# An MLP's down product by Strassen's seven products in place of eight, inside a fused RWKV-7 + MLP kernel

## The chip, the cores and the metric

The kernel runs on one core of one Trainium2 chip. The metric is the device time of one execution in microseconds: 678.31 us is the median of three runs of the kernel before (677.22 to 678.55). Engines are named as in the profile: PE (TensorE, matmul), PEld (its weight loads), DVE (VectorE), ACT (ScalarE), POOL (GpSimd), SP (the queue that issues all DMAs here). SBUF is the working memory, PSUM the memory that PE writes.

## The reference

Two stages. The first is a recurrence over 768 steps for 4 batches and 8 heads of 40 channels; its output is laid out as x with 3072 rows (batch and step) and 320 columns (head and channel). The second is an MLP.

```python
for t in range(S):
    y[:, :, t] = einsum('bhd,bhde->bhe', rt, state)
    Sa = einsum('bhde,bhe->bhd', state, at)
    state = state * wt[:, :, None, :] - einsum('bhd,bhe->bhde', Sa, bt) + einsum('bhd,bhe->bhde', vt, kt)
h = x @ w_in                        # 3072x320 @ 320x2048
g = h * sigmoid(1.702 * h)
out = g @ w_out                     # 3072x2048 @ 2048x320
```

All is float32.

## The kernel before

**Units and chunks.** The sequence is cut into 12 chunks of 64 steps. A chunk has two units (two batches each), 24 units in all. For a unit the kernel loads its inputs (`load`, `load_w`), forms the decays (`logarithm`, `decay`; the running sums are two DVE scans, L533 and L534), prepares score matrices (`prep`), inverts a triangular matrix level by level (`inverse`: PE product ps_level; copies W, L751; differences E, L753; transposes, L702 and L723; block spreading, L709 on POOL or DVE, L707 on ACT) and solves and carries the state (`solve`). Its output x, formed at L953 by four products on DVE or POOL, goes to DRAM (L963) and comes back transposed as xT_all (L967). The attention of unit i needs the state of the chunk before, so it is a chain; the MLP of a chunk only needs that chunk's two units.

**The MLP of a chunk.** x of the chunk has 256 rows: row blocks p (two pairs of batches) and b (batch of the pair). `up` makes h transposed, 2048 by 256, in four quarters q; each quarter is 2 x 5 tasks of four matmuls on the four 64x64 quarters of the PE array (`QUARTERS`), 256 columns wide. One ACT instruction (L988) applies the gelu to a quarter and writes g. `down(p)` then accumulates, for each p, 8 parts (m) of 2 x 4 matmuls with 64 columns of g as weights and 320 columns of w_out moving; row half r of the array writes its own PSUM bank r. A copy of bank 0 (L1012, ACT or DVE) and an add of bank 1 (L1014, DVE) give `ob`, which SP stores (L1011). Each float32 matmul of the code shows as two MATMULs and two LDWEIGHTS in the trace; all matmuls have line L300, the helper `mm`.

**PSUM** is used as four pairs of two banks; a task's number behind the engine's letter in the order is its pair. `down(0)` and `down(1)` are two different uses of a pair.

**Weights.** w_in and w_out come as eight 64-bit pieces of 1.31 MB, in four DMAs each (L469), and are rounded to float32 by an ACT, three DVE and one POOL instruction (L447 to L463). Raw pieces wait in `extra`, in not yet used parts of `w_sb`, or in xT_all.

**The order.** Nothing schedules at run time. Each task is added to a `Plan` with the engines that may do it and a cost for each; a task with `"sbuf": True` reads two SBUF operands and may stand on DVE or POOL or on DVE alone. The text `ORDER` names, for every task, its place, its engine (p, a, d, g, s for PE, ACT, DVE, POOL, SP) and its PSUM pair. `listed` reads it, and the tasks are issued in that order; every engine works through its own in sequence.

The buffers that matter: `g` has four slots (one chunk), `ob` one, x one, xT three.

Of the kernel before, what the change touches and what calls it, by code (L numbers as in the profile page):

```python
# [20 lines left out]
ALU = mybir.AluOpType  # L21
# [86 lines left out]
0s 8s 26s 5s 7s 9s 3a 6s 87p0 88p1 24s 89a1 1s 2s 12s 102a 95d 100p2 90a0 93d 158a 101d2 98p3 96g 10s 94d 17s 97g 16s 99d3  # L108
103p1 4a 11s 132p0 104a1 105d1 142p2 143p3 133a0 106d 130p1 14s 144a3 13s 107p0 15s 18s 151g 108a0 109d0 51s 131a1 110p3 27s
149g 150d 111a3 112d3 159p0 156p1 145a2 161d0 160a0 152g 113p3 345s 92a 162d 25s 153d 114a3 163p2 42s 115d3 34s 19a 274s 264p0  # L110
165d2 265p3 164a2 22d 266a3 166p2 20d 273s 21d 33s 43s 167a2 154p3 168d2 23g 35s 28a 157d1 116p2 155d3 169p1 117a2 118d2 267a0
279d 63s 280g 119p3 277s 171d1 36s 44s 123a3 120d3 343s 125d3 121a 278g 124d3 29d 287a 126p2 170a1 288p0 127a2 30d 172p1 479s
122a3 31d 289a0 128p2 54s 173a1 45s 129d2 32g 62s 174d1 134p3 37a 290d0 175p2 344s 135d3 180a2 146s 178a2 275s 176d2 136p1
179a2 38d 181a2 39d 177a 282g 276s 291d 91s 138a1 182p0 188p3 281d 183a0 186p2 139d 137a1 283p0 187a2 184p1 189a3 40d 140s
292p2 46a 60s 284d0 41g 285p3 185d1 148a 286d3 190p0 293a2 294d2 334p1 335p3 357a 191d0 141s 268g 147s 336a3 315d 192p2 47d
337a1 348d 316p0 194a2 346s 295p3 349d 61s 317a0 195g 347s 358p1 296a3 297d3 360d1 318a0 298p3 271a 361d 319p0 338g 300d3 196s
193a2 320a0 355p2 385d 270s 48d 299a3 362p0 356d2 351g 301p3 363a0 364d0 350g 386p2 197s 302d3 365p0 387a2 269s 352g 359a1
303d3 388a2 323p1 367d0 366a0 321p3 49d 324a1 304p2 322a3 478s 325d1 50g 353p0 309a2 470p3 354d0 209p1 307a2 210p1 310a2 305d2
211p1 308a2 272d 198p0 341a 199p0 72s 212p1 70s 64a 200p0 340s 368p2 52s 342d 339s 69s 201p0 369a2 202p0 370d2 203p0 471a
213p1 65d 214p1 389p2 66d 472a3 483g 204p0 390a2 560s 371p3 67d 306a 53s 215p1 71s 482s 216p1 372a3 217p1 476a 220p2 373d3 68g  # L120
218p1 221p2 477d 219a1 205p0 222p2 206p0 223p2 224p2 78s 559s 207p0 55a 311p3 225p2 79s 312d3 80s 226p2 208a0 58d 313p1 374p3
314d1 227p2 56d 379a3 228p2 229p2 57d 326p0 230a2 59g 393p1 327d0 378a3 391p2 394a1 375d3 231p0 558s 392d2 376a 232p0 233p0
395d1 81s 73a 234p0 480s 381p2 235p0 474s 328p1 475s 382a2 74d 377a3 485d 380a3 236p0 75d 481s 492a 242p2 486d 243p2 82a 76d
484d 77g 383p3 237p0 384d3 244p2 329d1 330d1 488p3 473d 238p0 531d 245p2 487g 246p2 489d3 85d 532p1 708s 239p0 533a1 396p3
331d 534a1 240p0 247p2 397d3 332s 241a0 562s 535p1 83d 490p3 536a1 84d 398p0 706s 572a 491d3 86g 550p1 253p3 399d0 551a 555s
400d0 561s 333s 254p3 401d 255p3 552a1 564d 493p0 402s 556a 567g 570p1 554s 494d0 248p2 705s 563d 566g 249p2 495d0 498d 256p3
571d1 565g 403s 250a2 496a0 251d2 696p1 497g 557d 539p0 252s 537p2 257p3 538a2 704s 540d0 701s 258p3 553d 611d 697a 499d 573p2
259p3 576a2 574d2 784s 710d 700s 260p3 787s 541d0 575d2 404p0 578d 261a3 577g 405p0 579d 698a1 568p2 711g 500p1 406p0 569d2
501a1 407p0 262d3 580p2 702a 502d1 263s 408p0 582d2 409p0 503d 410p0 583d 504a 612p3 411p0 584g 613d3 412p0 614d3 413p0 505p1
709d 414a0 426p3 506d1 427p3 428p3 507d1 429p3 699d 581d2 430p3 615p1 703d 431p3 616a1 785s 585p0 432p3 508d 586a0 433p3 587d0  # L130
434p3 509a 588d 435p3 589d 448p2 436a3 510p1 590p0 511a1 449p2 592d0 591a0 512d1 415p3 513d 416p3 593d 514a 417p3 594g 418p3
515p0 419p3 516a0 517d0 595p1 518d 420p3 596a1 597d1 421p3 598d 422p3 519a 599d 423p3 424p3 520p0 425a3 437p1 521d0 438p1
523d0 522g 439p1 524d0 440p1 525d0 441p1 442p1 526d0 527p3 718p0 528a3 443p1 719d0 929s 444p1 720d0 529p3 445p1 721d0 446p1
530d3 600p0 723d 447a1 542p3 722d 724g 603d0 605a0 619p1 604d0 543d3 450p2 620a1 606d0 544p3 621d1 601d0 602d 617p1 707s 546d3
451p2 618a1 783s 712d 547g 713d 607p0 725p1 608a0 452p2 609p0 453p2 548s 610d0 932s 454p2 727d1 726d1 622p0 728d 545d3 729a
775p1 455p2 623d0 780s 776a 549s 756d 730p3 624p0 456d2 457d2 731d3 458s 459p2 777a1 778g 732d3 786s 788g 781a 779s 626d0
460p2 625d0 627g 733d 795p1 835d 734a 461p2 735p3 791g 462p2 628s 736a3 796d1 737d3 716p0 792g 738d 463p2 782d 739g 1011s
920p1 757p3 925s 464p2 717d0 758a3 629s 759a3 790d 465p2 740p0 789d 466p2 741a0 742d0 921a 797p3 467d2 760p0 1008s 468d2 800a3
923d 652p2 469s 761d0 922a1 653p2 926a 930s 798d3 714p1 799d3 654p2 924s 802d 801g 655p2 934d 803a 656p2 836p0 657p2 715d1
658p2 659p2 837d0 762p3 838d0 927d 660p2 763a3 661p2 764p1 662a2 743d 630p0 744d 928s 631p0 632p0 765d1 804p3 766d1 633p0  # L140
805a3 806d3 634p0 807d 635p0 808a 745p2 636p0 748d2 637p0 749d2 839p1 933g 750d2 638p0 840a1 1009s 751d2 639p0 809p3 746d2
935g 640a0 641p1 810d3 642p1 793p2 747a 811d3 674p0 812d 794d2 813a 752p3 643p1 753a3 814p2 644p1 815a2 816d2 754p3 645p1
755d3 646p1 817d 647p1 818a 767p2 841p3 768d2 648p1 842a3 649p1 819p2 650p1 820a2 821d2 769p3 822d 651a1 823d 675p0 771d3 931s
770d3 772g 824p2 936d 676p0 827a2 828a2 942p1 829a2 677p0 1153s 830a2 937d 945a1 773s 663p3 825d2 664p3 943d1 1156s 826a 665p3
944d1 999p2 947d 946g 666p3 1000a 1004s 980d 940p1 948g 667p3 941d1 668p3 774s 669p3 670p3 831p1 671p3 1001a2 1002d 1003s
832d1 672p3 1005a 1013d 678p0 673a3 1006d 833p2 843p1 679p0 834d2 1007s 844d1 938p2 845d1 680p0 939d2 846p3 681p0 847d3 949p1
1012g 682d0 848p2 950a1 683d0 1014d 684s 685p3 849d2 1015g 1010s 850d2 1021p0 1016g 951d1 686p3 1024a0 1232s 851d 1235s 981p2
687p3 982a2 952d 852s 1022d0 983a2 953g 1144p1 1023d0 688p3 1026d 1145a 1149s 1025d 1027g 984p2 1059d 689p3 1154s 954p0 853s
985a2 1147g 690p3 1158d 1148s 955a0 956d0 986p2 1146a1 957d 1150a 691p3 958d 987a2 1151d 988p0 692p3 989a0 1152s 990d0 959p1
693a3 865p2 960a1 694d3 866p2 961d1 867p2 695s 962d 868p2 963d 1028p0 869p2 1029a0 1030d0 870p2 1031d 1157g 871p2 1159d 1032a  # L150
1060p3 872p2 873p2 1061a3 874p2 1062d3 1033p1 875a2 854p0 1035d1 855p0 1036d 856p0 1037d 1063p3 857p0 1064d3 1034a1 858p0
964p2 859p0 965a2 966d2 1038p1 967d 860p0 1039a1 1040d1 861p0 1041d 1017p3 968a 1042g 862p0 1018d3 863p0 969p2 864a0 876p1
970d2 877p1 972d2 971g 1043p3 973d2 878p1 1044a3 974d2 879p1 975d2 880p1 881p1 1045d3 1019p0 1046d 976p2 1047a 882p1 1020d0
1233s 883p1 977a2 1166p3 884p1 1169a3 1167d3 1377s 978p0 885p1 1168d3 898p2 1171d 1170g 886a1 979d0 887p3 1172a 1048p0 991p1
1051a0 888p3 1052a0 992d1 889p3 1053a0 890p3 1054a0 891p3 1049d0 993p1 1050a 1067p0 994d1 1160g 1155s 892p3 1161d 1068a0 893p3
894p3 1069d0 1380s 895p3 1204d 1065p0 995d1 896p3 996d 1066a0 1231s 1055p1 899p2 897a3 1056d1 997s 1173p0 1223p3 900p2 1174a0
1175d0 1228s 1176d 1224a 1177g 1057p1 901p2 1058d1 1070p0 998s 1164p1 1225a3 1226d 1236g 1227s 1071d0 902p2 1229a 1165d1
1162p3 903p2 1238d 1163d3 904p2 1237d 1178p0 1230d 905p2 1179a0 1180d0 1245p1 906a2 1181d 1072p3 1248a1 1456s 907d2 1182g
1246d1 908s 1247d1 909p0 1250d 1234s 1239g 1073d3 1251a 910p0 1240g 1074d3 1249d 1183p2 1459s 1283d 1368p1 911p0 1184a2 1075d
1373s 912p0 1185d2 1369a 1076s 1186d 1252p3 1187d 913p0 1370a1 1371g 1372s 1382d 1253a3 1188p2 1254d3 1374a 914p0 1255d 1190d2  # L160
1256g 1077s 1189a2 1191d 1243p1 1375d 915p0 1192g 1257p3 916p0 1244d1 1258a3 1259d3 1205p2 917d0 1206a2 1193p1 918d0 1207a2
# [87 lines left out]
def rwkv7_gelu_quick(ctx: ExitStack, tc: tile.TileContext, time_d, v_d, w_d, wc_d, ak_d, b_d, rv_d, w_in, w_out, out):  # L249
# [3 lines left out]
    C = 64  # L253
# [11 lines left out]
    PLAIN = 4  # L265
    PARTS = 4
    ROUNDS, WINDOW, SHARE = 4, 5000.0, 1.0
    RANKS = [14, 16, 20, 24, 35, 37, 39, 41]
    HALF = [slice(0, 64), slice(64, 128)]
    CHANNELS = [slice(h.start, h.start + D) for h in HALF]  # L270
    BITS = (0, 1)
# [858 lines left out]
```

## Time and profile before

| | before |
|---|---|
| median of three runs | 678.31 us (677.22 to 678.55) |
| span of the profiled execution | 681.1 us, 2.8 above that median |
| MATMULs of ps_down, 64x320 | 3072, mean 430 ns, union 240.3 us |
| MATMULs of ps_up, 64x256 | 3840, mean 377 ns, union 254.4 us |
| ACT gelu, L988 | 48, mean 1024 ns |
| ACT table loads | 30, 1283 ns each |
| POOL L709 (128x512) | 29, mean 1323 ns; DVE the same 699 ns |
| first ps_up, first ps_down | 69.0, 93.5 us |
| DMA | 69.73 MB, mean 102 GB/s |

How to read it: the busy time of a group is the union of its instructions' spans. Matmuls are pipelined, so that a span of 430 ns says little about how often one can start; the distance from start to start in the timeline says that. A share of busy time is a mean over the whole span, and the stretches of this kernel differ.

### The profile page before, as it was taken

What the parts mean: (1) busy time and instruction counts of PE and PEld (TensorE: products, weight loads), DVE (VectorE), ACT (ScalarE), POOL (GpSimd) and SP (SyncE); (2) the same over time, 40 slices, a digit from 0 to 9 for tenths busy, and PEclk for the clock granted to TensorE, in tenths of its full rate; (3) what the DMA queues carried; (4) which work ended last, traced back from release to release, by engine and by line L of the source; (5) the groups of instructions that cost most, each with busy time, mean ns of one, the idle gap of its engine ahead of it and who ended that gap; (6) DMA issues with size and microseconds to landing.
All of it is one profiled execution on the core that took longest, in us unless ns stands there. A gap on an engine that the chain in (4) does not pass through costs nothing.

```text
span 681.1 us, 42181 instructions
## 1 busy us (share of the span) xinstructions
PE 652.0 (96%) x19488; PEld 572.4 (84%) x19488; DVE 445.5 (65%) x906; ACT 330.7 (49%) x688; POOL 176.7 (26%) x204
## 2 busy tenths in 40 slices
PE   5777999999999999999999999999999999999997
PEld 5667888997987788888888898899899799889996
DVE  4687877777867668767776587868556766675001
ACT  4675845544564654664545445455454354252110
POOL 5443444225123123123123211321412421300000
PEclk9788999999999999999999999999999999999999
DMA  7874755205314314432404413513502312200100
GB/s 235 275 244 148 228 158 173 89 14 155 108 50 139 103 45 125 124 108 67 121 23 131 140 34 107 154 33 106 149 29 71 121 51 58 58 13 23 51 12 21
DMA packets 35312, 69.73 MB, mean 102 GB/s; under 512 B 5440, under 2 KB 14656, under 8 KB 35136
## 3 DMA queue, kind: packets, MB, share of 16 engines
q1 hardware_dynamic: 35136, 67.03, 32.8%
q8 instruction: 153, 2.51, 1.6%
q14 instruction: 23, 0.19, 0.1%
HBM read 59.15 MB, written 7.86 MB: 98 GB/s over the span
## 4 chain that ended last, share of the span: by engine, by line
PE 91%; DMA 4%; ACT 1%; DVE 1%; issue 1%; SPq 0%; ACTq 0%; DVEq 0%
PE ps_up L300 31%; PE ps_down L300 30%; PE ps_level L300 9%; PE ps_y L300 5%; PE ps_B L300 4%; PE ps_X L300 2%; PE ps_N L300 2%; PE ps_rz L300 2%; PE ps_RV L300 2%; PE ps_A L300 1%; DMA ak<-in_ak 1%; PE ps_zT L300 1%; PE ps_Q L300 1%; DMA time<-in_time 1%; PE ps_T L300 1%
## 5 line engine op out<-in xcount | busy, mean ns | idle before, releaser
L300 PE MATMUL ps_up<-xT_all,w_sb 64*64 64x256 f32 x3840 | 254.4, 377 | 2.0 <-DMA xT_all<-x_dram 1.1
L300 PE MATMUL ps_down<-w_sb,g 64*64 64x320 f32 x3072 | 240.3, 430 | 1.1 <-issue 0.9
L300 PEld LDWEIGHTS ps_up<-xT_all,w_sb 64*64 64x64 f32 x3840 | 172.9, 133 | 17.7 <-issue 2.5
L300 PEld LDWEIGHTS ps_down<-w_sb,g 64*64 64x64 f32 x3072 | 143.3, 133 | 31.4 <-issue 1.6
L988 ACT ACTIVATE g<-ps_up 128x1024 f32<-128x1024 f32 x48 | 49.1, 1024 | 44.7 <-PE ps_up L300 44.3
L709 POOL TENSOR_TENSOR EX<-ES,quads 128x512 f32<-128x512 f32 x29 | 38.3, 1323 | 115.5 <-DVE ES L702 83.1
L751 ACT COPY W<-ps_level 128x512 f32<-128x512 f32 x56 | 32.7, 585 | 69.1 <-PE ps_level L300 67.4
L300 PEld LDWEIGHTS ps_level<-W,EX 64*64 64x64 f32 x2560 | 59.2, 134 | 5.8 <-DVE T L830 0.2
L300 PE MATMUL ps_level<-W,EX 64*64 64x64 f32 (+1 forms) x2560 | 56.2, 217 | 0.0
L753 DVE TENSOR_TENSOR E<-two,ps_level 128x256 f32<-128x256 f32 x80 | 33.1, 415 | 34.7 <-ACT W L751 30.7
L707 ACT ACTIVATE EX<-ES,quads 128x256 f32<-128x256 f32 x80 | 36.3, 501 | 30.4 <-DVE ES L702 29.9
L619 POOL TENSOR_TENSOR ak<-ak,FT 128x512 f32<-128x512 f32 x16 | 22.0, 1378 | 76.2 <-DMA ak<-in_ak 54.4
L300 PE MATMUL ps_level<-PT,EX 64*64 64x64 f32 (+2 forms) x1280 | 34.9, 244 | 5.7 <-DVE EX L723 4.8
L300 PEld LDWEIGHTS ps_level<-PT,EX 64*64 64x64 f32 x1280 | 32.6, 145 | 8.9 <-DVE EX L723 5.7
L702 DVE STREAM_TRANSPOSE ES<-E 128x256 f32<-128x256 f32 x80 | 35.2, 442 | 4.7 <-DVE E L753 0.5
L300 PE MATMUL ps_y<-M,bh 64*64 64x104 f32 (+1 forms) x768 | 34.8, 247 | 1.3 <-DVE M L907 0.8
L300 PE MATMUL ps_y<-RV,kh 64*64 64x104 f32 (+1 forms) x768 | 34.9, 247 | 0.3 <-DVE EX L723 0.3
L891 ACT COPY B<-ps_B 128x416 f32<-128x416 f32 (+1 forms) x34 | 16.5, 492 | 33.5 <-PE ps_B L300 33.2
L300 PEld LDWEIGHTS ps_y<-RV,kh 64*64 64x64 f32 x768 | 28.9, 133 | 2.0 <-DVE M L907 0.5
L907 DVE TENSOR_TENSOR M<-ps_X,later 128x832 f32<-128x832 f32 (+1 forms) x24 | 23.8, 993 | 9.8 <-PE ps_X L300 9.5
L627 POOL TENSOR_TENSOR kh<-time,G 128x320 f32<-128x320 f32 x18 | 16.2, 902 | 48.4 <-PE ps_y L300 34.4
L300 PEld LDWEIGHTS ps_y<-M,bh 64*64 64x64 f32 x768 | 27.0, 133 | 1.9 <-DVE M L907 1.2
(131 smaller groups left out, 1097.2 us busy)
## 6 DMA issues: line engine op xcount, KB each, us to landing
ak<-in_ak SPq DMA_DIRECT2D x48, 160.0 KB
rv<-in_rv SPq DMA_DIRECT2D x48, 160.0 KB
time<-in_time SPq DMA_DIRECT2D x24, 320.0 KB
xT_all<-x_dram SPq DMA_DIRECT2D x48, 160.0 KB
wc<-in_wc SPq DMA_DIRECT2D x20, 264.0 KB
logw<-in_w SPq DMA_DIRECT2D x24, 160.0 KB
RV<-in_v SPq DMA_DIRECT2D x24, 160.0 KB
b<-in_b SPq DMA_DIRECT2D x48, 80.0 KB
```

Source lines behind the costliest of these rows:

```text
L300: nc.tensor.matmul(o, lhsT, rhs, start=start, stop=True, skip_group_check=True)
L619: plan.add(R, {"DVE": 690.0, "POOL": 1270.0, "sbuf": True}, lambda t: of(t.engine).tensor_mul(ahT(), ahT(), FT_of(i)), reads=T("ak", "FT") ...
L627: plan.add(R + 4, {"POOL": 870.0, "DVE": 490.0, "sbuf": True}, lambda t, n=n, dst=dst: of(t.engine).tensor_mul(dst(i)[:, :, :D], by_head(t ...
L702: plan.add(rank, dve(256), lambda t: nc.vector.transpose(ES(n), source(t)), writes=[key("ES", n, 6)], **reads)
L707: nc.scalar.activation(dst[:, :, h], ES(n), ACT.Copy, scale=quads[:, h, :1])
L709: of(t.engine).tensor_mul(dst, ES(n).unsqueeze(2).to_broadcast([128, 8, 2, 32]), quads.unsqueeze(1).to_broadcast([128, 8, 2, 32]))
L751: plan.add(rank, any2(512), lambda t: copy(t.engine)(tiles_of(W(n + 1)), blocks(psum(t, ""), 64)), writes=[key("W", n + 1, 5)], pair=pair)
L753: plan.add(rank, dve(256), lambda t: nc.vector.tensor_sub(tiles_of(E(n + 1)), every(two32, [128, 2, 4, 32]), blocks(psum(t, ""), 64)[:, :, ...
L891: plan.add(R, any2(4 * wide), lambda t: copy(t.engine)(dst(), some(psum(t, "")[:, :, :208])), writes=[("Bv", i)] if x and c > 0 else T("B" ...
L907: plan.add(R + 1, dve(8 * wide), lambda t: nc.vector.tensor_tensor(M_of(i)[:, :, :wide].rearrange("p (j b) n -> p b j n", b=2), some(psum( ...
L988: plan.add(-45, {"ACT": 1030.0, "table": "gelu"}, lambda t: nc.scalar.activation(g_of(c * NQ + q).rearrange("p m r n -> p r m n"), psum(t, ...
```

## The change

The down product of a chunk is a product of a 2x2 block matrix (rows by p, inner dimension by the parity of the 128-row block f) with a 2x2 block matrix of w_out (inner by parity, 320 columns in two halves of 160). Before, it took eight block products. Now it takes seven, each 160 columns wide, in the variant of Strassen's scheme with shared sums:

- `forms` makes, once, four sums of blocks of w_out: T1 in place, T2 in a new tile `mixed`, T3 and T4 in `extra`; four tasks for each of the four w_out pieces, on POOL or DVE.
- `mix` makes, for each quarter of g, three sums on POOL or DVE: S1 and S3 in one instruction of 512 elements, S2 and S4 of 256 each. A g tile grows from 4 to 7 blocks of 128 columns.
- `down(s)` is two halves that share one PSUM pair. Each part has three block products by four matmuls. In half s, row half r of the array takes the products of bank r ^ s, so that over both halves each bank gets both row halves' sums. A tiny copy of PSUM (`fence`, ACT or DVE) after half 0 is waited for by half 1.
- `down4` makes the seventh product in another pair, 8 parts of four matmuls.
- `combined` forms the four output blocks: one copy of 480 columns, adds of 320 and 160 from PSUM, two SBUF sums (POOL or DVE), two adds from the other pair, and two stores. The results lie in `extra`, behind the weights' raw pieces.

`ORDER` is wholly new: 3004 tasks in place of 2700, with other engines for many of the old tasks, another order of the loads at the start, and other PSUM pairs. The DMA scratch of the program is set to 1024.

```diff
-  A=1, ... x=1, xT=3, g=4, ob=1), 4)
+  A=1, ... x=1, xT=3, g=4, mix=1, ob=1), 4)
+    mixed, fence = single("mixed", [128, NM * HD]), single("fence", [128, 2])
...
+    extra_forms = extra[:, 2 * PIECE:].rearrange("p (k m c) -> p k m c", k=2, c=HD)
+    w_forms = w_out_sb.rearrange("p (m j k c) -> p m j k c", j=2, k=2, c=HD)
+    B11, T1, B21, B22 = (w_forms[:, :, j, k] for j, k in product(BITS, BITS))
+    T2, T3, T4 = mixed.rearrange("p (m c) -> p m c", c=HD), extra_forms[:, 0], extra_forms[:, 1]
+    def forms(n, rank):
...
+        for name, dst, a, b, op, reads in (("T3", T3, B22, T1, ALU.add, ...),
+                                           ("T1", T1, T1, B11, ALU.subtract, ...),
+                                           ("T2", T2, B22, T1, ALU.add, ...),
+                                           ("T4", T4, B21, T2, ALU.subtract, ...)):
...
-    g_of = lambda n: buf("g", n, [128, 2, 2, 256])
+    g_of = lambda n: buf("g", n, [128, 2, 7 * 128])
+    PRODUCTS = [((0, B11), (5, T2)), ((1, T1), (6, B22)), ((2, B21), (4, T3))]
...
+        def mix(q):
...
+            for name, size, dst, a, b in (("S13", 512, ...), ("S2", 256, ...), ("S4", 256, ...)):
+                plan.add(-44, {"POOL": ..., "DVE": ..., "sbuf": True}, ... tensor_sub(dst(), a(), b()), ...)
...
-                    for f in (2 * m, 2 * m + 1):
+                    for i, both_of in enumerate(PRODUCTS):
                         for r, b in QUARTERS:
-                            o = p * 128 + b * 64
-                            mm(po[HALF[b], r, :DM], g[HALF[r], f % 2, o:o + 64], w_out_sb[HALF[r], f * DM:(f + 1) * DM], f == 0)
+                            k = r ^ s
+                            form, w = both_of[k]
+                            mm(po[HALF[b], k, i * HD:(i + 1) * HD], F[HALF[r], form, b * 64:b * 64 + 64], w[HALF[r], m], s == 0 and m == 0 and i == 0)
...
+            if s == 0:
+                plan.add(R + 18, {"ACT": 215.0, "DVE": 160.0}, lambda t: copy(t.engine)(fence, psum(t, "")[:, :, 0]), ... writes=[("turn", c)], ...)
+        def down4():
...
+                    for r, b in QUARTERS:
+                        mm(po[HALF[b], r, :HD], F[HALF[r], 3, b * 64:b * 64 + 64], T4[HALF[r], m], m == 0)
...
+        def combined():
...
-        for p in BITS:
-            down(p)
+            mix(q)
+        down(0)
+        down4()
+        down(1)
+        combined()
```

## Prediction

> **What bounds the kernel now.** I began with the page's head and its chain of waits.
>
> ```profile
> span 681.1 us, 42181 instructions
> PE 652.0 (96%) x19488; PEld 572.4 (84%) x19488; DVE 445.5 (65%) x906; ACT 330.7 (49%) x688; POOL 176.7 (26%) x204
> PE 91%; DMA 4%; ACT 1%; DVE 1%; issue 1%; SPq 0%; ACTq 0%; DVEq 0%
> ```
>
> TensorE carries 91% of the chain, so work taken from it counts. An average hides stages, so next came the table of busy time by stretch (columns: stretch; busy us and count of PE, PEld, DVE, ACT, POOL; granted clock; DMA share; GB/s).
>
> ```profile
> 0.00:17.00 17.00, 9.48 (x248) 8.56 (x248) 7.90 (x14) 6.99 (x25) 9.91 (x42) 1.00 0.80 235
> 17.00:34.00 17.00, 12.10 (x412) 10.90 (x416) 10.86 (x16) 10.46 (x21) 8.03 (x6) 0.80 0.84 275
> 34.00:51.00 17.00, 12.53 (x489) 11.25 (x486) 14.26 (x28) 13.14 (x33) 7.48 (x4) 0.90 0.77 244
> 51.00:68.00 17.00, 13.24 (x542) 12.16 (x532) 12.44 (x18) 9.71 (x25) 6.47 (x11) 0.90 0.49 149
> 68.00:102.00 34.00, 32.41 (x872) 28.37 (x867) 26.67 (x40) 22.38 (x47) 14.14 (x6) 1.00 0.62 193
> 408.00:476.00 68.00, 68.00 (x2142) 59.26 (x2138) 51.94 (x106) 34.50 (x77) 15.53 (x15) 1.00 0.34 100
> ```
>
> There are two regimes. In the **head**, up to the first MLP matmul at 69.0 us, PE has gaps: DMA, DVE and their hand-overs set the pace (DVE busy 7.90+10.86+14.26+12.44 = 45.5 of 68). From then on PE is full, and DVE at 51.94/68 = 76% has room. In the head PE matters little; behind it only PE does.
>
> Busy time of a matmul group is a union of pipelined spans, not its cost. The timeline of PE gives the cost by start to start.
>
> ```profile
> 203.74 0.45 PE L300 MATMUL ps_cum<-logw,edges 64*64 64x160 f32 x8
> 204.01 0.61 PE L300 MATMUL ps_up<-xT_all,w_sb 64*64 64x256 f32 x8
> ...
> 206.63 0.41 PE L300 MATMUL ps_Q<-T,P 64*64 64x64 f32 x16
> 206.86 1.05 PE L300 MATMUL ps_up<-xT_all,w_sb 64*64 64x256 f32 x16
> 207.73 1.26 PE L300 MATMUL ps_down<-w_sb,g 64*64 64x320 f32 x16
> 208.81 0.41 PE L300 MATMUL ps_T<-QT,Tc 64*64 64x64 f32 x16
> ```
>
> Call the four quarter-array matmuls that run together a pass. Each matmul of the code is two instructions here, so two passes. 320 columns: 16 instructions = 4 passes in 208.81-207.73 = 1.08 us, 0.270 a pass. 160 columns (ps_cum): 2 passes in 0.27, 0.135. 64 columns (ps_Q): 4 passes in 0.23, 0.058. 256 (ps_up at 204.01, followed by other work at 204.44): 0.216. Priced so, all passes of the program sum to 630 us before and, counted in the new order, 606 after.
>
> **Parts of the change.**
>
> *Matmuls.* A chunk's down product is 2 row pairs x 8 m x 2 f x 2 = 64 passes of 320 columns: 64 x 0.270 = 17.3 us. The new one is 2 x 8 x 3 x 2 = 96, and 8 x 2 = 16 for the fourth form, 112 passes of 160: 112 x 0.136 = 15.2. The difference is 2.0 us; 12 chunks give **-23.9**. Weight loads rise from 3072 to 5376. If the four loads of a pass came one after another at the 58 ns of the narrow pass, 0.23 a pass would bind and 1344 passes would cost 309 us, not 183; but that row holds four loads *and* four matmuls in 58 ns, so 160 columns cover them.
> [...]
>
> *Sums of g.* Three per quarter chunk, 144 tasks. In the new order 79 stand on POOL (24 of 512 elements, 55 of 256) and 65 on DVE (24 and 41). Rows: POOL 128x512 L709 median 1.28, 128x256 L697 0.73; DVE 0.69 and about 0.42 (L753). So POOL +24 x 1.28 + 55 x 0.73 = 71, DVE 16.6 + 17.2 = 34.
>
> *Evacuation.* The 24 copies and 24 adds of 320 leave (DVE 9 x 0.49 + 24 x 0.48 = 16 gone). Per chunk a copy of 480, an add of 320 and three of 160 that read PSUM, and two SBUF adds come. On DVE: 4 x 0.65 + 12 x 0.48 + 36 x 0.34 + 7 x 0.48 + 6 x 0.33 = 26, with fences 27. Weight forms: 16 sums, ten on DVE at 0.47 (5 us).
>
> *New order.* Counting each engine's rows, DVE also takes over copies and products (11 W, 10 P, 13 B, 7 QT, 8 kh and small ones, about +26); ACT sheds some 30, and six table loads of 1.283 (7.7). DVE: 445.5+34-16+27+5+26 = about **522**; POOL 177+71+11 (eight EX, one T)+8 (evacuation)+5 (forms)-6 = **266**; ACT about 291. ACT's gain is worth nothing, as it bounds nothing.
>
> *The head.* It is not the same head. Ahead of the second chunk-0 x read the SP queue now issues 18.7 MB, not 14.9; before the first up matmul DVE has 36 more instructions (8 weight steps, six scans, copies, inverses), at some 0.65 about +23 us, and PE has 40.5 us of passes ahead, not 32.4.
>
> ```profile
> 59.06 1.10 SPq L967 DMA_DIRECT2D xT_all<-x_dram  x2
> ```
>
> 14.9 MB by 60.2 us is 247 GB/s; 18.7 MB is then issued by 75.6, and with the same 10 us to the first up matmul it starts at 85.5: 16.5 later, less 8.1 of PE work done ahead, +8.4. From DVE: first down matmul was at 93.3 with 62 us of DVE and 56 of PE listed ahead; now 89.5 and 61. If DVE fits the extra 27 in at full rate beside nothing, +27-5 = +22; if it fills the 22.5 us in which it idled in the first 68, 0. I take **+11**, near the DMA row and the middle.
>
> *Fences.* Between the halves PE waits for a tiny read of PSUM on ACT or DVE (rows: L581 0.200, L797 0.21, plus the matmul's drain 0.296-0.034 = 0.26). The first half's successor on PE is 0.8 to 5.3 us of other passes, under 1.7 in eight chunks; behind the fence the next half and its evacuation queue. Free if covered, up to 1 us each with a DVE instruction in front: 0 to 12, I take **+2**.
>
> *Store and tail.* [...]
>
> ```profile
> 661.91 14.32 PE L300 MATMUL ps_down<-w_sb,g 64*64 64x320 f32 x208
> ...
> 676.27 0.49 DVE L1012 COPY ob<-ps_down 128x320 f32<-128x320 f32 x1 [7.60 <-PE ps_down L300]
> 676.79 0.49 DVE L1014 TENSOR_TENSOR ob<-ob,ps_down 128x320 f32<-128x320 f32 x1
> ```
>
> Last PE to last DVE is 1.0 us now. Then: copy of 480 on ACT 0.56, and on DVE 0.48+0.34+0.48+0.34+0.34, of which five fourth-form parts (5 x 0.27) hide 1.4: 1.6, **+0.6**. The last gelu and its three sums (1.02+0.69+0.42+0.73 and hand-overs) lie under 4.1 us of down passes listed before the first that needs them.
>
> *Locks between DVE and POOL.*
>
> ```profile
> L533 DVE TENSOR_TENSOR_SCAN wc<-starts,wc x20: 666/700/3175, 70.3 to 540.3; 128x264 f32<-128x264 f32 x20
> L953 DVE TENSOR_TENSOR x<-zr,FT x56: 274/282/928, 46.9 to 630.2; 128x128 f32<-128x128 f32 x56
> ```
>
> Minimum, median, maximum: a DVE instruction with two SBUF inputs at times takes a whole POOL instruction longer, while those that read PSUM (L753, 415 with and without POOL beside) never do. Summed over groups, what DVE took beyond its medians is 20 us, POOL 11. POOL's load rises by 1.5 and the DVE tasks of that kind from 185 to 281, also 1.5: the excess should double, DVE +20 to +25. Behind the head it is hidden as long as DVE keeps up with PE; I take **+3** of PE waits there.
>
> **Sum**, against the profiled 681.1: -23.9+11+2+0.6+3 = -7.3, so 673.8. The median of the runs (678.31) is 2.8 below the span: **671.0**.
>
> **Rivals.**
> 1. *Everything added is hidden.* The head's extra DVE work slides into idle time, fences are covered. For it: ACT and POOL are under half busy, DVE idled a third of the head. Against: 3.8 MB more ahead. 681.1-23.9+0.6 = 657.8, 655 as a median. Chance 0.17.
> 2. *DVE becomes the bound, slower than before.* Behind the head DVE must do (522+22-89-10)/(606-61-40) us of work per us of PE passes until attention ends: 445/505 = 0.88, against 0.76 now. A queue in strict order that waits for locks and for PSUM results was never above 26.67/34 = 0.78 in any stretch shown. Held at 0.78, the 505 us become 445/0.78 = 570; with a PE of 1.5% overhead they would be 513, so +57; held at 0.84, +17, and against -23.9+11+2.6 the sum is +7: 688, 685 as a median. It decides from a DVE share of about 0.85. For it: the lock excess; against: much of the work is free to wait, since only attention feeds on DVE closely. Chance 0.25 (slower 0.19, same 0.05, faster 0.01).
> [...]
> 3. *The weight loads bind after all* at something between 0.136 and 0.23 a pass; at 0.16 1344 passes cost 32 us more: 706. The ps_cum row is against it. Chance 0.03, slower.
>
> The forecast, head and small waits eating about two thirds of the saving (664 to 677), has 0.55; 0.03 of it lies within 0.2%. Together faster 0.17+0.52+0.01 = **0.70**, same **0.08**, slower **0.22**; 0.2% is about what a measurement here can tell. **Range** 656 to 686: from rival 1 to the nearer part of rival 2; the forecast's own is 662 to 677.
>
> **What would show it.** Start to start, 24 ps_down instructions in 0.82 us (else rival 3). First ps_up near 85 us. Behind that, PE at 99%: if stretches with PE below 95% and DVE above 85% appear, rival 2. L533 and L953 means well above 871 and 307. A last-store tail longer by half a microsecond. I am wrong if the head costs nothing, or if PE waits for the sums or the fences by more than 10 us.

## The result, and the profile after

The median of four runs is 756.7 us (754.7 to 758.7), beside 678.4 us for the kernel before on the same chip: a ratio of 1.114 (95% interval 1.109 to 1.119). The change makes the kernel slower by 78 us, where 7 us less was forecast. The head of the page after and its chain of waits:

```profile
span 756.9 us, 46954 instructions
PE 665.3 (88%) x21792; PEld 601.9 (80%) x21792; DVE 526.0 (69%) x1063; ACT 292.4 (39%) x619; POOL 277.4 (37%) x302
PE 68%; DVE 11%; DMA 10%; issue 7%; POOL 2%; ACT 1%; SPq 1%; DVEq 0%; POOLq 0%; ACTq 0%
```

DVE, ACT and POOL came out as counted (522, 291 and 266 were worked out). TensorE fell from 91% of the chain to 68%, and "issue", time in which an engine waited for nothing that the profile shows, rose from 1% to 7%. The table by stretch (columns as in the prediction) says where:

```profile
68.00:102.00 34.00, 22.39 (x743) 19.55 (x743) 31.24 (x45) 17.81 (x41) 15.30 (x13) 0.75 0.49 158
272.00:340.00 68.00, 63.69 (x2127) 58.20 (x2118) 49.12 (x109) 24.65 (x53) 24.71 (x25) 0.97 0.27 77
408.00:476.00 68.00, 60.80 (x2115) 55.19 (x2106) 52.05 (x110) 28.89 (x61) 24.66 (x24) 1.00 0.32 97
```

Two things are new. The head is still going on between 68 and 102 us: PE is busy for 22.39 of 34, where the kernel before had 32.41. And behind the head PE is no longer full: 60.80 and 63.69 of 68 in place of 68.00, while DVE stands at 52.05 from 408 to 476 us, hardly more than the 51.94 of before. The stretch of the kernel before from 272 to 340 us, which was not shown yet:

```profile
272.00:340.00 68.00, 68.00 (x2106) 56.85 (x2102) 49.38 (x101) 38.17 (x76) 16.96 (x18) 1.00 0.36 106
```

What PE waited for between 136 and 716 us (columns: matmul; what ended the wait; us in total, times, longest):

```profile
PE ps_down L317 <- issue: 9.3, 15, 1.7
PE ps_y L317 <- issue: 4.9, 7, 1.0
PE ps_X L317 <- issue: 3.5, 5, 1.7
PE ps_up L317 <- DMA xT_all<-x_dram: 3.0, 2, 1.6
```

The waits behind no semaphore sum to 34 us in that view, those for DVE to 3. Before, between 136 and 640 us, there was a single one:

```profile
PE ps_y L300 <- issue: 0.5, 1, 0.5
```

One part of the page plays no part in the prediction: the list of DMA queues, where q8 carries instructions. The first line is of the kernel before:

```profile
q8 instruction: 153, 2.51, 1.6%
```

The same line of the kernel after:

```profile
q8 instruction: 171, 2.80, 1.6%
```

The columns are packets, MB, share. 2.80 MB in 171 packets is 16384 bytes each. PE has 38976 instructions (matmuls and weight loads) before and 43584 after, and 38976/153 and 43584/171 are both 255; the experiments below keep to this (45120 with 177 packets, 37440 with 147). So nearly all packets are PE's, at about 256 instructions each. A pass of 160 columns takes 0.136 us, and holds eight instructions (four loads, four matmuls): 256 instructions last 4.35 us. A pass of 64 columns takes 0.058: 256 last 1.86 us. I cut each trace into blocks of 256 PE instructions and set the time that their passes need (the prices of the prediction) beside the time they took. Behind the first 34 blocks:

| blocks whose passes need under 3.3 us | number | need, mean | took, mean |
|---|---|---|---|
| before | 6 of 120 | 3.14 | 3.13 (all six lie above 3.0) |
| after | 56 of 138 | 2.92 | 3.58 |

The first theory followed: **PE's instructions come in blocks of 256 and not faster than about one in 3.5 us (theory F).** The rivals: DVE, GpSimd and the sums hold PE up (L); the new order does so, in its head (H) or behind it.

### The profile page after: what moved, and what is told of

It reads as the page before. It is cut to its first block, busy times and chain, and to the rows that moved or that the text cites. A ratio compares the mean times of both kernels' runs of the same rounds, so it can differ in the third digit from the quotient of the medians.

```text
span 756.9 us, 46954 instructions
## 1 busy us (share of the span) xinstructions
PE 665.3 (88%) x21792; PEld 601.9 (80%) x21792; DVE 526.0 (69%) x1063; ACT 292.4 (39%) x619; POOL 277.4 (37%) x302
## 4 chain that ended last, share of the span: by engine, by line
PE 68%; DVE 11%; DMA 10%; issue 7%; POOL 2%; ACT 1%; SPq 1%; DVEq 0%; POOLq 0%; ACTq 0%
PE ps_up L317 23%; PE ps_down L317 19%; PE ps_level L317 7%; PE ps_B L317 4%; PE ps_y L317 4%; PE ps_four L317 3%; DMA rv<-in_rv 2%; DMA ak<-in_ak 2%; PE ps_X L317 2%; DMA xT_all<-x_dram 1%; PE ps_rz L317 1%; PE ps_A L317 1%; PE ps_RV L317 1%; PE ps_N L317 1%; DMA x_dram<-x 1%
## 5 line engine op out<-in xcount | busy, mean ns | idle before, releaser
L317 PE MATMUL ps_down<-w_sb,g 64*64 64x160 f32 x3072 | 190.4, 298 | 7.7 <-issue 7.6
L317 PEld LDWEIGHTS ps_down<-w_sb,g 64*64 64x64 f32 x3072 | 159.8, 133 | 12.9 <-issue 12.2
L1036 POOL TENSOR_TENSOR g<-g 128x256 f32<-128x256 f32 (+1 forms) x79 | 73.5, 933 | 100.0 <-DVE g L1036 57.3
L317 PE MATMUL ps_down<-extra,g 64*64 64x160 f32 x768 | 101.9, 298 | 1.2 <-issue 1.2
L317 PE MATMUL ps_down<-mixed,g 64*64 64x160 f32 x768 | 101.0, 299 | 0.6 <-issue 0.5
L744 POOL TENSOR_TENSOR EX<-ES,quads 128x512 f32<-128x512 f32 x37 | 49.1, 1328 | 73.5 <-DVE ES L737 60.0
L317 PEld LDWEIGHTS ps_down<-extra,g 64*64 64x64 f32 x768 | 67.1, 133 | 3.1 <-issue 3.1
L317 PEld LDWEIGHTS ps_down<-mixed,g 64*64 64x64 f32 x768 | 61.4, 134 | 1.6 <-issue 1.2
L1036 DVE TENSOR_TENSOR g<-g 128x256 f32<-128x256 f32 (+1 forms) x65 | 39.8, 617 | 22.8 <-ACT g L1026 15.0
L317 PE MATMUL ps_four<-extra,g 64*64 64x160 f32 x768 | 37.4, 298 | 1.4 <-issue 1.3
```

What stands on the lines that cost most here:

```text
L317: nc.tensor.matmul(o, lhsT, rhs, start=start, stop=True, skip_group_check=True)
L744: of(t.engine).tensor_mul(dst, ES(n).unsqueeze(2).to_broadcast([128, 8, 2, 32]), quads.unsqueeze(1).to_broadcast([128, 8, 2, 32]))
L1036: plan.add(-44, {"POOL": 180.0 + 2.14 * size, "DVE": 170.0 + 1.03 * size, "sbuf": True}, lambda t, dst=dst, a=a, b=b: of(t.engine).tensor_ ...
```

## Experiments

Ratios are to the kernel before, run on the same chip beside each. Kernels whose products are cut or replaced say so in their expectation. The two kernels with a stream of their own (probe_before, probe_full) were executed once each, and only their streams are read.

**1. Instruction supply alone.** The kernel before with each matmul of 320 columns as two of 160; the order, the sums and every other engine stay.

```diff
-  for r, b in QUARTERS:
+  for h, (r, b) in product((0, 160), QUARTERS):
...
-    mm(po[HALF[b], r, :DM], ..., w_out_sb[HALF[r], f * DM:(f + 1) * DM], f == 0)
+    mm(po[HALF[b], r, h:h + 160], ..., w_out_sb[HALF[r], f * DM + h:f * DM + h + 160], f == 0 and h == 0)
```

> The kernel before, with each down matmul of 320 columns made as two of 160: the same columns on PE, the same order and the same work on the other engines, but 45120 PE instructions in place of 38976. Theory F (PE's instructions are fetched in blocks of 256 and a block cannot take less than about 3.4 to 3.6 us, so short passes starve PE): the order has 72 blocks behind the head whose passes sum to less than 3.5 us, in place of 18, and their shortfall is 24 us in place of 3; so 15 to 35 us slower, 693 to 715, with PE idle in the middle of streams with no releaser. [...] Theory H (the new order's head and nothing else): no change.

Measured: 737.4 us, 1.082 (1.077 to 1.088). The passes need 2 us more; the kernel became 55 us slower. What PE waited for behind its head:

```profile
PE ps_down L300 <- issue: 22.0, 29, 1.7
```

Of its blocks 45 need under 3.3 us; their mean need is 3.04, and they took 3.75. F holds, though the size was beyond its range; L and H would have left this kernel as it was. These 45 blocks make up 32 of the 55 us, so a floor for the shortest blocks alone does not give the size.

A stricter sign is where in the row of instructions PE stands. If all PE instructions of a trace are counted in order, those that wait on semaphores included, a supply of blocks of 256 must show at one place of each 256. It does. Behind 136 us, all 54 waits of split_before that no semaphore ends (those above 0.15 us, 33 us together) lie at number 193 or 194 of 256, and so do 54 of the 55 in the kernel after. By start-to-start distances, 51 of the 58 us that split_before loses there lie at this place, which I call the block edge.

Then streams of their own behind the kernel's work: matmuls with no semaphores and no data traffic, of 64, 96, 128 and 160 columns, with 320 columns ahead of each.

> The kernel before, and behind it, when nothing else runs, long streams of matmuls into a PSUM pair that nobody reads: 96 calls by four quarters of 320 columns ahead of each of 384 of 64 columns, 256 of 96, 256 of 128 and 256 of 160. Theory F: the first some thousand instructions of a stream run at 58, 83, 110 and 136 ns a pass, then the 64-column stream falls to about 8 instructions in 106 to 112 ns (256 in 3.4 to 3.6 us), so does that of 96, and 128 and 160 columns are at or above that and keep their speed. Theories L and H: 58, 83, 110 and 136 throughout.

The timeline of PE in the 64-column stream (start, length, instructions, idle before):

```profile
726.45 2.10 PE L300 MATMUL probe<-w_sb 64*64 64x64 f32 x128 [1.09 <-issue]
730.19 2.10 PE L300 MATMUL probe<-w_sb 64*64 64x64 f32 x128 [1.65 <-issue]
733.66 2.10 PE L300 MATMUL probe<-w_sb 64*64 64x64 f32 x128 [1.38 <-issue]
737.68 2.10 PE L300 MATMUL probe<-w_sb 64*64 64x64 f32 x128 [1.92 <-issue]
```

128 matmuls and their 128 loads, 256 instructions, run in 2.10 us; ahead of each 256 PE stands, in these rows for 1.09 to 1.92 us. Start to start it is 3.47 to 4.02 us, 3.70 in the mean of 22 blocks: 0.115 us a pass. With 96 columns it is 3.73 (0.116 a pass) and with 128, whose passes themselves need 3.49, it is 3.59 (0.112); with 160 every block takes the 4.35 of its passes. All 38 waits lie at number 193 of 256, the edge found above. Only the first 174 matmuls of the 64-column stream, with their loads some 350 instructions and not the thousand of the expectation, ran unhindered, so little more than one block is held ahead.

**2. The same in the kernel after: fewer, wider matmuls.** In place of three matmuls of 160 columns two of 240, and then one of 480; sums, order and columns stay.

```diff
-  for i, both_of in enumerate(PRODUCTS):
-    for r, b in QUARTERS: ... mm(po[HALF[b], k, i * HD:(i + 1) * HD], F[HALF[r], form, ...], w[HALF[r], m], ...)
+  for r, b in QUARTERS:
+    mm(po[HALF[b], r ^ s, :480], F[HALF[r], 6, ...], w_out_sb[HALF[r], m * 640:m * 640 + 480], ...)
```

> The changed kernel with the three products of 160 columns of a part made as two of 240: the same 480 columns on PE and the same bank, a third fewer down instructions (40512 PE instructions in place of 43584), everything else as it was. It leaves the seven-product arithmetic out: the operands are not the right blocks. Theory F: the shortfall behind the head goes from 35 to 21 us, so 10 to 25 us faster than the changed kernel, 732 to 747. Theory L: within 4 us of 757. Theory H: within 4 us of 757.

> The changed kernel with the three products of a part as one of 480 columns: the same columns and bank, 37440 PE instructions in place of 43584 (the version with two of 240 had 40512). It leaves the seven-product arithmetic out. Theory F: the shortfall behind the head falls from 35 to 12 us by the same count that gave 21 with 240; so 20 to 35 us faster than the changed kernel, 722 to 737. [...]

Measured: 749.2 us, 1.097 (1.093 to 1.101), just outside F's range, and 732.4 us, 1.075 (1.070 to 1.080), inside it. With three, two and one matmul a part the kernel takes 757, 749 and 732 us, and 50, 29 and 22 us are lost at block edges behind 136 us. So supply is worth 24 us or more in this kernel. But the last one has 37440 PE instructions, fewer than the kernel before, and still loses 50 us: F is not all.

**3. The sums of g.** The kernel after with each sum cut to 2 columns.

> The changed kernel with the three sums of g made over 2 columns each and the products reading g itself in place of the sums: the same instructions in the same order, but some 100 us of DVE and GpSimd work and all waits for the sums gone. It leaves the sums out. Theory L: most of the 78 us comes back, below 700. Theory F: the idle time of PE with no releaser behind the head stays near 50 us, and the time falls only by what the head and the named waits hold, 5 to 30 us, 725 to 752. Theory H: 5 to 20 us from the head.

Measured: 764.0 us, 1.117 (1.110 to 1.122): nothing gained. F had expected 725 to 752, so that was a miss too; L, under 700, falls as the main cause. In the 480-column form, where PE is better fed, the same cut was made:

> The same with the sums of g over 2 columns and no product waiting for them; sums and seven-product arithmetic are left out. Theory F with the sums harmless: the same as the version with 480 columns alone, within 6 us. Theory L beside F: a further 15 us and more.

Measured: 723.1 us, 1.059 (1.055 to 1.064), 9 less than with the sums, between the two expectations. They do cost something, once PE waits less for instructions.

**4. Fewer instructions by the whole array.** One 128x128 matmul in place of four on quarters; full_after keeps all seven products. The edit of full_before:

```diff
-  for r, b in QUARTERS: ... mm(po[HALF[b], r, :DM], g[HALF[r], f % 2, o:o + 64], w_out_sb[HALF[r], ...], f == 0)
+  mm(po[:, f % 2, :DM], g[:, f % 2, p * 128:(p + 1) * 128], w_out_sb[:, f * DM:(f + 1) * DM], f < 2)
```

> The changed kernel, still with all seven products, but the three products of a part each as one matmul of 128 rows by 128 columns of weights in place of four on quarters of the array: half s of the down product then fills bank s alone. The order is as it was; PE's instructions fall from 43584 to 36672. Theory F (PE's instructions arrive at 256 in about 3.6 us alone and 3.9 beside other transfers): nearly all blocks behind the head are then longer than that; the idle time of PE with no releaser there goes and 40 to 55 us come back, 700 to 717; what stays above the kernel before is the head. A rival, M: a full-array matmul costs more than its quarter passes or must wait when the array changes between whole and quarters; then the gain is smaller than 25 us, or there is a loss.

> The kernel before with the down product by full-array matmuls of 128 by 128 by 320 (even f into bank 0, odd f into bank 1); 34368 PE instructions in place of 38976. Theory F: the shortfall behind the head is only 3 us, so 0 to 6 us faster, 676 to 682. Rival M: slower by the cost of every change between whole and quarters, some 190 down parts and as many returns: 10 us and more.

> The kernel before, and behind it streams of full-array matmuls of 320, 160 and 80 columns, then 64 pairs of one quarter pass set and one full matmul at 320, and 64 at 160. If a full matmul costs what four quarters cost, 0.54, 0.27 and 0.14 us each, and the pairs 1.08 and 0.54. Rival M: more, or the pairs more than the sum of their parts.

Measured: 750.1 us, 1.097 (1.089 to 1.105), for full_after, and 728.0 us, 1.065 (1.057 to 1.073), for the kernel before in this form. PE of full_before, start to start:

```profile
316.57 1.34 PE L300 MATMUL ps_down<-w_sb,g 128*128 128x320 f32 x4
317.85 0.69 PE L300 MATMUL ps_rz<-rv,zT 40*64 40x64 f32 x32
318.47 1.34 PE L300 MATMUL ps_down<-w_sb,g 128*128 128x320 f32 x4
```

The four matmuls take 1.28 us, not the 1.08 of the sixteen, and the ps_rz behind them 0.62, not 0.465: 0.36 us for going to the whole array and back. The stream of pairs gave the same: a pair of one quarter group and one whole matmul took 1.43 us with 320 columns, where the work is 1.08, and 0.90 with 160, where it is 0.54. In a stream of its own a whole matmul cost what four quarters cost (0.54 with 320 columns, 0.27 with 160; with 80 it took 0.22, not 0.14). full_before goes to the whole array in 142 stretches: 142 x 0.36 = 51 us, beside the 46 it lost. full_after has 117 of them, 42 us, while its loss at block edges fell from 50 to 15 us: what the smaller count of instructions gave back, the changes took.

**5. Seven products in the order of before.** I put the seven products, on the whole array, into the order of the kernel before, the down parts in batches of 8 or 4 to save array changes.

> All seven products, by full-array matmuls, but in the order of the kernel before: its head, its attention and its up tasks stand as they did; the eight parts of a half of the down product are put together in one run (26 runs in all), the fourth form goes with the first half, each half has its own PSUM pair as before and no fence; sums of g on GpSimd. Theory F with H: PE's passes are 26 us less than before, 26 changes to the full array and back cost 0.36 each (9 us), instructions are too few to starve PE, and the head is the old one: 682-26+9 = 665, with 5 us of new waits 665 to 672. [...]

> The same in runs of four parts (45 runs). By the price of a change, 19 more of 0.36 us, 7 us slower than with runs of eight, unless the shorter runs spare waits of the attention: 670 to 680.

Measured: 804.2 us, 1.177 (1.169 to 1.184), and 749.4 us, 1.099 (1.095 to 1.103): both expectations missed by far. (L had been given 682 us or more for the first.) The waits of PE in seven_b4 behind 136 us:

```profile
PE ps_X L310 <- DVE T L858: 4.3, 4, 1.6
PE ps_level L310 <- POOL EX L737: 3.7, 3, 1.8
```

"Issue" is 2.0 us there, but waits for DVE sum to 19, for ACT to 8, for POOL to 4. A likely reason, not tested, is that down parts are also the filler between the steps of the attention chain, and that gathered they leave those steps without cover. These two runs change several things at once. One thing more can be read from them: with the head of the order before, their first up matmul is at 69.5 and 70.6 us, though they have the sums of w_out and the DMA scratch of 1024.

**6. The order alone.** In order_eight PE does the columns of eight products again, in the new order, with all sums; order_alone also cuts all sums to 2 columns.

```diff
  (from the 480-column kernel)
-  mm(po[HALF[b], r, :HD], F[HALF[r], 3, ...], T4[HALF[r], m], m == 0)
+  mm(po[HALF[b], r, :DM], F[HALF[r], 3, ...], w_out_sb[HALF[r], m * 640:m * 640 + DM], m == 0)
  (order_alone, beside that; its products read g itself)
-  out=dst[:, some], in0=a[:, some], in1=b[:, some], op=op)
+  out=dst[:, some, :2], in0=a[:, some, :2], in1=b[:, some, :2], op=op)
-  tensor_sub(dst(), a(), b())
+  tensor_sub(dst()[..., :2], a()[..., :2], b()[..., :2])
```

> The kernel after, its order, its sums and its fences, but TensorE does the column work of eight products again: each part is one matmul of 480 columns per quarter and each part of the fourth form 320 columns instead of 160; 37440 TensorE instructions, fewer than the 38976 of the kernel before (the products are not Strassen's: it leaves out the right operands). If the count of instructions were all (instruction supply, theory F alone), this is the kernel before: 678 to 690. If the new order has a cost of its own, the head of 31 us later plus some 15 to 25 us in which TensorE waits for producers or meets runs of narrow matmuls: 722 to 740. If the new order costs in its head alone: 708 to 716.

> The run above with all sums of g and of w_out cut to 2 columns, so that nearly nothing of the new DVE and GpSimd work is left, but the same order (it leaves out the sums). If the sums of w_out make the later head and the sums of g the waits behind it: 685 to 700. If it is the order itself (loads, scans and copies listed in other places): within 15 us of the run above, 710 to 730.

Measured: order_eight 744.7 us, 1.095 (1.089 to 1.101); order_alone 728.3 us, 1.072 (1.064 to 1.080). The first lies a little above what was expected of an order with a cost of its own (722 to 740), the second inside its 710 to 730. F alone falls with the first, and the second says that most of the loss needs neither Strassen's matmuls nor its sums: with the matmul columns of before, the new order is 48 us slower. The fences, the new evacuation and the PSUM pairs are still in order_alone, so "order" below includes them. Two stretches of order_alone:

```profile
68.00:102.00 34.00, 21.65 (x734) 19.24 (x729) 30.86 (x45) 17.44 (x39) 14.92 (x12) 0.75 0.49 155
408.00:476.00 68.00, 62.90 (x1880) 48.02 (x1876) 48.63 (x111) 29.79 (x65) 16.95 (x21) 1.00 0.31 91
```

The same poor head, and PE not full behind it. For the whole set I summed what PE needs for its passes, and what lies between starts beyond that. "At edges" is the part of the loss behind 136 us that lies at block edges (numbers 188 to 199 of each 256). What is missing to the span, 8 to 10 us, lies ahead of the first matmul and behind the last:

| us | PE instructions | passes need | lost up to 136 us | lost behind | at edges | time |
|---|---|---|---|---|---|---|
| before | 38976 | 631 | 36 | 5 | 1 | 678 to 682 |
| split_before | 45120 | 633 | 38 | 58 | 51 | 737 |
| order_alone | 37440 | 630 | 60 | 29 | 11 | 728 |
| order_eight | 37440 | 630 | 65 | 37 | 15 | 745 |
| one480 | 37440 | 605 | 63 | 53 | 22 | 732 |
| after | 43584 | 607 | 66 | 74 | 50 | 757 |

Read downwards from order_alone: the order costs 24 us in the head and 24 behind it; the sums 5 and 8; seven products need 25 us less, of which 16 come back as losses behind the head, 7 of them at block edges; three narrow matmuls in place of one wide cost another 21 behind the head, with 28 more at the edges and 7 less elsewhere. These 37 take the whole saving of 25 and 12 us more: 757 against 745. In the kernel after, supply is thus the largest single loss behind the head, 50 of 74 us, and 10 of the 24 that the order adds there are supply too.

**7. The head.** First the sums of w_out alone:

> The kernel after with only the sums of w_out cut to 2 columns (it leaves them out; its products take other blocks). If they are what DVE and GpSimd spend the head on: first up matmul at 85 to 95 instead of 102, time 742 to 750. If the head is later through the loads' order and the DVE work listed ahead: first up matmul near 100, time 752 to 760.

Measured: 753.0 us, 1.107 (1.101 to 1.113), first up matmul at 102.2 (102.5 in the kernel after): they don't make the head. Then the DVE steps that round the weights, since DVE was busy for 80.6 of the 102.4 us ahead of the first up matmul, and for 46.1 of 69.0 before:

```diff
-  nc.vector.tensor_single_scalar(scale(), scale(), 3, op=ALU.logical_shift_left)
+  nc.vector.tensor_single_scalar(scale()[:, :64], scale()[:, :64], 3, op=ALU.logical_shift_left)
   ... and likewise in the two other steps
```

> The kernel after with the three DVE steps of rounding each weight piece cut from 1280 to 64 columns (so most weights are not rounded, and DVE has 21.2 us of work less ahead of the first up matmul). If DVE is what makes the head (it is busy 80.6 of the 102.4 us there): first up matmul at 82 to 90, time 738 to 748. If the place of the loads or the chain through TensorE and ACT makes it: first up matmul at 97 to 102, time 750 to 758.

> The same cut in the kernel before (11.2 us of DVE work less ahead of its first up matmul, where DVE was busy 46.1 of 69.0 us). If DVE does not bind that head, the first up matmul comes 0 to 4 us earlier (65 to 69) and the time is 674 to 682; if it binds there too, 58 to 61 and 668 to 672.

Measured: 759.2 us, 1.114 (1.109 to 1.119), and 681.9 us, 1.002 (0.999 to 1.005). In light_before the first up matmul came at 72.3 us, 3 later and not 0 to 4 earlier. The first up matmul of light_after, with DVE at 70.1 of the first 102 us:

```profile
97.76 9.74 PE L317 MATMUL ps_up<-xT_all,w_sb 64*64 64x256 f32 x176
```

It is 5 us earlier, not 13 to 20, and the time is no shorter. DVE did have a part in it, since the second read of x was issued 6 us earlier (76.7 for 83.0), but 5 of 21 us is little, and not much above noise: in split_before and full_before, which share the head of the kernel before, the first up matmul is at 66.9 and 69.2 us. So neither the sums of w_out nor DVE's load of rounding makes the head; the high share of DVE did not mean that DVE was its bound. What remains is the place of the tasks. The stores of x and its transposed reads on SP, after:

```profile
52.05 0.68 SPq L998 DMA_DIRECT2D x_dram<-x  x2
54.24 1.21 SPq L1002 DMA_DIRECT2D xT_all<-x_dram  x2
80.78 0.67 SPq L998 DMA_DIRECT2D x_dram<-x  x2
82.97 1.09 SPq L1002 DMA_DIRECT2D xT_all<-x_dram  x2
```

And the two stores before:

```profile
47.79 1.54 SPq L963 DMA_DIRECT2D x_dram<-x  x2
56.42 0.68 SPq L963 DMA_DIRECT2D x_dram<-x  x2
```

In the kernel before, x of chunk 0's second unit is stored 8.6 us after the first's, in the kernel after 28.7 us (and 28.7 in order_alone): the two units no longer run interleaved. Then 19.5 us pass from its read to the first up matmul instead of 10. In the lists, 69 PE tasks stand ahead of that matmul, not 55, and PE works in order. The first up matmul at 69.5 and 70.6 us in run 5, where the order of before is kept, agrees with this; but no run moved these tasks alone, so which of them sets the head is read from the lists and the trace, and not shown.

## Why the prediction was wrong, point by point

- **The matmuls (-23.9): the step that failed.** Its sum of passes was right: 607 us after for the 606 counted, and the start-to-start distance came true:

```profile
700.66 0.30 PE L317 MATMUL ps_down<-w_sb,g 64*64 64x160 f32 x1
...
701.48 0.30 PE L317 MATMUL ps_down<-w_sb,g 64*64 64x160 f32 x1
```

That is 24 matmuls in 0.82 us. What the step left out is that passes need instructions: it priced each by its columns and weighed the loads, not the supply. The runs showed in its place that 50 us are lost behind the head at block edges, where the kernel before loses 1. "160 columns cover them" holds for a row of such passes (4.35 us a block in the stream of 160), and fails where narrower passes of the attention stand in the same block (56 blocks of the kernel after need 2.92 us in the mean and took 3.58). The step also took the new order's neighbourhoods for granted: a PE that was full before would be full after.
- **The head (+11).** Right in kind, mis-sized: +30 us lost up to 136 us. The DMA term failed at two points: the second read was issued at 83.0, not 75.6, and the "same 10 us to the first up matmul" were 19.5. The outer bound from DVE, +22, came nearer for a wrong reason, as run 7 shows. The clock is a small part at most: it was granted at half for 44 of the first 136 us, 14 in the kernel before, and the passes in these stretches, which need 15 and 7 us at full clock, took about 1.85 times that (0.107 us in place of 0.058 at 64 columns), an estimate of 7 us more.
- **"From then on PE is full".** Carried over from the order of before. With the matmul columns of before, the new order leaves 29 us of gaps behind its head in place of 5: a term of 24 us that had no price at all. Of the 29, 11 lie at block edges, the supply again. The trace of order_alone names the hand-over of transposed x (3 us) and DVE results (3 us) for a part of the rest; what makes the remainder stays open.
- **The sums of g and the DVE and POOL loads.** Counts right (526, 277, 292). Their cost in waits, put at +3, is 9 us (one480) to 16 us (order_eight, with the sums of w_out) in the kernels where PE is better fed, and nothing to be seen in the kernel after itself. What the prediction calls locks, DVE instructions that last longer beside one of POOL, grew as said; the lines of the kernel after:

```profile
L569 DVE TENSOR_TENSOR_SCAN wc<-starts,wc 128x264 f32<-128x264 f32 x20 | 19.6, 981 | 0.0
L988 DVE TENSOR_TENSOR x<-zr,FT 128x128 f32<-128x128 f32 x56 | 16.6, 355 | 0.2
```

That is 981 and 355 ns in the mean, from 871 and 307. The longest L569, at 63.68 us, took 3.42 us and ended 0.57 us behind POOL's L481, which had started 0.46 us ahead of it and took 3.30. The excess of DVE over its medians went from 20 to 44 us; a growth of 20 to 25 was forecast.
- **Fences and tail.** Behind 136 us no wait of PE for a fence is seen, where +2 was put. From the last matmul to the end it is 5.7 us, from 4.9: +0.8, where +0.6 was put.
- **Rival 1 (everything hidden).** Only the covered fences of it held: the head's extra work did not fit into idle time, and PE's gaps behind it are new.
- **Rival 2 (DVE as the bound).** Slower is what came, but not by this: DVE's share behind the head hardly rose (0.72 from 136 to 680 us, from 0.69 between 136 and 640), no stretch behind 102 us reached 0.85, and removing the sums of g gained nothing in the kernel after. DVE's instructions beside POOL's did get longer, as above; that DVE thereby becomes the bound was an estimate of the prediction, and it did not happen.
- **Rival 3 (the weight loads).** Its sign and its count, 2304 more loads, pointed near the right thing; its mechanism, a price a pass, is not what happened: the passes kept 0.136 us, and the loss lies at block edges. At 0.03 it was held too unlikely because the ps_cum row has only two passes in it, far fewer than the 32 that use up a block.
- **The range.** Its upper end knew only DVE. No rival had the order itself as its mechanism, though all 2700 tasks were listed anew, as 3004.

## What to carry to other kernels

Count instructions beside columns: on a full TensorE, see whether the passes of 256 instructions (matmuls and weight loads) need less than the 3.6 to 3.7 us that such a block took here (3.58 in the mean of 56 blocks of the kernel after, 3.70 in the stream of 64 columns), since a change that trades columns for more and narrower matmuls can lose more in supply than it wins in passes (here 50 us at block edges, for 24 us of passes). Price a new order as a change of its own, by when the first consumer's last input is issued and by what is listed ahead of it, before pricing what it carries. And test a high busy share by cutting that work: here a DVE that was busy for 79% of the head bounded next to nothing.

## What the runs showed of the hardware that was not expected

- In the 64-column stream of probe_before, without other traffic, TensorE's instructions came 256 at a time, 3.47 to 4.02 us apart, and little more than one block ahead (some 350 instructions ran before the first wait). A float32 pass on quarters took, in its long rows, 0.115 us at 64 columns (0.058 by its columns), 0.116 at 96 and 0.112 at 128; at 160 it took the 0.136 of its columns.
- A change from quarters to the whole array and back cost 0.36 us, with 320 and with 160 columns (1.43 for 1.08 us of work, 0.90 for 0.54).
- In the head of the kernel after, where PE is busy for 22.53 us of 34 (34 to 68 us) and for 22.39 (68 to 102 us), from 25.77 and 32.41 before, the granted clock was 0.72 and 0.75, from 0.90 and 1.00; a pass of 64 columns took 0.107 us at half clock, not 0.058.
